# Two blocks of a weight matrix loaded by transfers over five and three DMA engines, in a decode step of attention and a gated MLP

## The chip, the cores and the metric

The kernel runs on one NeuronCore of a Trainium2 chip. Its engines are TensorE (PE in the profile, with its weight loads as PEld), VectorE (DVE), ScalarE (ACT), GpSimd (POOL) and SyncE (SP), which issues nearly all transfers. Sixteen DMA engines move the data. The metric is the device time of one execution in microseconds, and smaller is better.

## The reference

One decode step for eight sequences. All arrays are float32.

```python
xn = layernorm(x)                                  # x: [8, 1, 512]
q = (xn @ wq) -> 32 heads of 128                   # wq: [512, 4096]
scores = q . k_cache * 128 ** -0.5                 # k_cache: [8, 8, 4096, 128], 4 query heads share a k head
o = softmax(scores) @ v_cache                      # v_cache: as k_cache
s = o @ wo                                         # wo: [4096, 512]
z = gelu(xn @ w_in)                                # w_in: [512, 1792]
z1, z2 = z[..., :896], layernorm(z[..., 896:])
y = (z1 * (w_sp * z2 + b_sp)) @ w_out              # w_out: [896, 512]
out = x + s * silu(y)
```

The caches make up most of the bytes: 16 loads of 8.4 MB for each of k and v.

## The kernel before

**Loads.** Every load but x is one or more transfers from SP's queue, in the order of the program, and each fills all 128 partitions. A ring of three slots of 64 KB for each partition (pool `ring`, `slot()`) takes them: the first slot holds `w_mlp` (w_in, the seven blocks of w_out and small side values, line 59), the second wq (line 74), and then come the k and v loads of each head in two halves (`load_k`, line 288, `load_v`, line 295). At the end come wo in ten transfers (lines 322 and 325) and the last half of v in two. A load into a slot waits until all reads of the slot's last content are done. x is a transfer of eight rows from ACT's queue (line 71), into the columns of the MLP's slot that its load leaves free. `from_slot` gives out these columns, and the MLP's temporaries lie there too.

**Work.** First comes the layer norm of x and its transpose `xnT` (lines 122 to 130). Then `mlp()` runs: products with w_in into `pz` (line 145), gelu, layer norm and gate on DVE (lines 148 to 177), two transposes into `hT` (line 181), and seven products, one for each block of 128 rows of w_out (line 186). Each of the blocks goes to one of four groups of 32 rows in PSUM, which `pick` adds (line 193), and a silu leaves the result in `gate` (line 201). `project_q` makes the queries in two quads of heads (line 208) and spreads them into `qz` (line 220). For each head then `scores` (line 231), `softmax` (lines 236 to 259) and `values` (line 273) run, each half as it lands. After the last head the last pieces of wo are used as they land (line 307 and, straight into the result, line 354), and the result is stored from ACT's queue (line 368).

**What sets the order.** Instructions run on each engine in the order of the program text. Semaphores stand between engines. Nothing in the program says which DMA engine takes which row of a transfer.

Of the kernel before, what the change touches and what calls it, by code (L numbers as in the profile page):

```python
# [8 lines left out]
F32 = mybir.dt.float32  # L9
# [4 lines left out]
P = 128  # L14
B, D = 8, 512
HKV, REP, S, DH = 8, 4, 4096, 128
NK = D // P
G = 4
J = S // (G * P)
R = 32  # L20
FH = 896
FQ = 256
NB = FH // P
EPS = 1e-5
GELU_C = 0.7978845608028654
HALF = B // 2
# [2 lines left out]
W = 64  # L29
# [5 lines left out]


@with_exitstack
def tile_gqa_gmlp_decode(ctx: ExitStack, tc: tile.TileContext, x, kT, v, wq, wo, w_mlp, out, gate, stored):
    nc = tc.nc
    head = ctx.enter_context(tc.tile_pool(name="head", bufs=1))  # L40
    l = head.tile([P, HKV], F32, name="l")
# [5 lines left out]
    work = ctx.enter_context(tc.tile_pool(name="work", bufs=1))  # L47
# [4 lines left out]
    def slot():  # L52
        return ring.tile([P, SLOT], F32, name="slot")


    mlp_slot = slot()
    n_in, n_out = NK * 2 * FH, NB * D
    n_mlp = n_in + n_out + P
    nc.sync.dma_start(mlp_slot[:, :n_mlp], w_mlp)
    w_in_sb = mlp_slot[:, :n_in].rearrange("p (k n) -> p k n", k=NK)  # L60
    w_out_sb = mlp_slot[:, n_in:n_in + n_out].rearrange("p (j d) -> p j d", j=NB)
    side_sb = mlp_slot[:, n_in + n_out:n_mlp]
    spare = [n_mlp]

    def from_slot(rows, n):
        lo = spare[0]
        spare[0] = lo + n
        return mlp_slot[:rows, lo:lo + n]

    x_sb = from_slot(B, D)  # L70
    nc.scalar.dma_start(x_sb, x)

    wq_sb = slot()
    nc.sync.dma_start(wq_sb, wq)
    wq_sb = wq_sb.rearrange("p (k n) -> p k n", k=NK)


    ident = const.tile([P, P], F32, name="ident")
# [31 lines left out]
    def scratch(shape, name):  # L110
        t = ps.tile([P, 512], F32, name="scr")
        n = 1
        for s in shape[1:]:
            n *= s
        return t[:shape[0], :n]
# [16 lines left out]
    x_out = const.tile([P, W], F32, name="x_out")  # L132

    def mlp():
        z = from_slot(P, 2 * FQ).rearrange("p (a f) -> p a f", a=2)
        u = from_slot(P, 2 * FQ).rearrange("p (a f) -> p a f", a=2)
        pz = scratch([P, 2 * FQ], "pz")
        nc.vector.memset(pz, 0.0)
        pz_v = pz.rearrange("p (a f) -> p a f", a=2)
        w_in_v = w_in_sb.rearrange("p k (a f) -> p k a f", a=2)  # L140
        for k in range(NK):
            for g in range(G):
                lo = g * FQ
                n = min(FQ, FH - lo)
                nc.tensor.matmul(pz_v[R * g:R * (g + 1), :, :n], xnT[:, k, :],  # L145
                                 w_in_v[:, k, :, lo:lo + n], start=(k == 0), stop=(k == NK - 1))
        zf, uf = z.rearrange("p a f -> p (a f)"), u.rearrange("p a f -> p (a f)")
        nc.vector.tensor_copy(zf, pz)
        nc.vector.tensor_mul(uf, zf, zf)
        nc.vector.tensor_scalar(uf, uf, 0.044715, 1.0, op0=ALU.mult, op1=ALU.add)  # L150
        nc.vector.tensor_mul(uf, uf, zf)
        nc.scalar.activation(uf, uf, AF.Tanh, scale=GELU_C)
        nc.vector.tensor_scalar(uf, uf, 1.0, 0.5, op0=ALU.add, op1=ALU.mult)
        nc.vector.tensor_mul(zf, uf, zf)

        def mean(src, name):
            part_sum = small.tile([P, 1], F32, name="part_sum")
            nc.vector.tensor_reduce(part_sum, src, op=ALU.add, axis=AX.X)  # L158
            pm = scratch([P, 1], "pm")
            nc.tensor.matmul(pm, same_all, part_sum, start=True, stop=True)  # L160
            t = small.tile([P, 1], F32, name=name)
            nc.vector.tensor_scalar(t, pm, 1.0 / FH, None, op0=ALU.mult)
            return t

        z1, z2 = z[:, 0, :], z[:, 1, :]
        mu = mean(z2, "mu")
        nc.vector.tensor_scalar(z2, z2, mu, None, op0=ALU.subtract)
        nc.vector.tensor_mul(u[:, 0, :], z2, z2)
        nc.vector.memset(u[(G - 1) * R:, 0, FH - (G - 1) * FQ:], 0.0)
        var = mean(u[:, 0, :], "var")  # L170
        nc.vector.tensor_scalar(var, var, EPS, None, op0=ALU.add)
        rs = small.tile([P, 1], F32, name="rs")
        nc.gpsimd.tensor_tensor(rs, var, neg_half, op=ALU.pow)
        nc.vector.tensor_scalar(z2, z2, rs, None, op0=ALU.mult)
        nc.vector.tensor_scalar(z2, z2, side_sb[:, W:W + 1], side_sb[:, W + 1:W + 2],
                                op0=ALU.mult, op1=ALU.add)
        nc.vector.tensor_mul(u[:, 1, :], z2, z1)
        hT = from_slot(P, 2 * P).rearrange("p (a s) -> p a s", a=2)
        for a in range(2):
            th = scratch([P, P], "th")  # L180
            nc.tensor.transpose(th, u[:, 1, a * P:(a + 1) * P], ident)
            nc.vector.tensor_copy(hT[:, a, :], th)  # L182
        pw = scratch([P, D], "pw")
        for j in range(NB):
            g, a = divmod(j, 2)
            nc.tensor.matmul(pw[R * g:R * (g + 1), :], hT[:, a, R * g:R * (g + 1)], w_out_sb[:, j, :],  # L186
                             start=(a == 0), stop=(a == 1 or j == NB - 1))
        y_sb = from_slot(P, D)
        nc.vector.tensor_copy(y_sb, pw)  # L189
        py = scratch([P, W], "py")  # L190
        for g in range(G):
            for a in range(2):
                nc.tensor.matmul(py[R * g:R * (g + 1), :], pick[:, a, :],  # L193
                                 y_sb[:, (2 * g + a) * W:(2 * g + a + 1) * W], start=(a == 0), stop=(a == 1))
        nc.vector.tensor_copy(x_out, side_sb[:, :W])
        e = from_slot(P, W)
        nc.vector.tensor_scalar(e, py, -1.0, 87.0, op0=ALU.mult, op1=ALU.min)
        nc.scalar.activation(e, e, AF.Exp)
        nc.vector.tensor_scalar(e, e, 1.0, None, op0=ALU.add)
        nc.vector.reciprocal(e, e)  # L200
        nc.vector.tensor_mul(gate, py, e)

    def project_q(quad):
        pq = scratch([P, REP * DH], "pq")
        for k in range(NK):
            for g in range(G):
                lo = (quad * G + g) * REP * DH
                nc.tensor.matmul(pq[R * g:R * (g + 1), :], xnT[:, k, :], wq_sb[:, k, lo:lo + REP * DH],  # L208
                                 start=(k == 0), stop=(k == NK - 1))
        q_sb = work.tile([P, REP * DH], F32, name="q_sb", tag="p")  # L210
        nc.vector.tensor_scalar(q_sb, pq, float(DH) ** -0.5, None, op0=ALU.mult)  # L211
        tq = scratch([P, REP * P], "tq")
        for r in range(REP):
            nc.tensor.transpose(tq[:, r * P:(r + 1) * P], q_sb[:, r * DH:(r + 1) * DH], ident)  # L214
        tv = tq.rearrange("p (r g c) -> p r g c", r=REP, g=G)
        for g in range(G):
            h = quad * G + g
            for b in range(B):
                o = b * R + b * REP
                nc.vector.tensor_copy(qz[:, h, o:o + REP], tv[:, :, g, b])  # L220
# [86 lines left out]
                nc.tensor.matmul(part[R * q:R * q + B, i * n:(i + 1) * n], oT[:, h, r, :],  # L307
                                 wo_sb[:, m, i * n:(i + 1) * n], start=(m < REP), stop=(cuts == 2))

    mlp()  # L310
    project_q(0)
    project_q(1)
    for h in range(HKV):
        for half in range(2):
            scores(h, half, load_k(h, half))
        pT = softmax(h)
        po = po_ps[:, h % 2]
        for half in range(2):
            last = h == HKV - 1 and half == 1
            if last:  # L320
                wo_slot = slot()
                nc.sync.dma_start(wo_slot[:, :WO_EARLY * D], wo[:, :WO_EARLY * D])
                v_sb = load_v(h, half, 2)
                for lo, hi in WO_PIECES:
                    nc.sync.dma_start(wo_slot[:, lo * D:hi * D], wo[:, lo * D:hi * D])
                wo_sb = wo_slot.rearrange("p (m d) -> p m d", d=D)
                project_o(0, WO_EARLY)
            else:
                v_sb = load_v(h, half, 1)
            n = 2 if last else HALF  # L330
            for i in range(0, HALF, n):
                done = values(half * HALF + i, n, pT, v_sb[:, i:i + n])
                if half or i:
                    combine(*o_prev, po)
                o_prev = done
        combine(*o_prev, po)
        po_t = po.rearrange("p (b r) -> p r b", r=REP)
        if h < HKV - 1:
            nc.vector.tensor_copy(oT[:, h], po_t)
        else:  # L340
            for a in range(2):
                nc.vector.tensor_copy(oT_last[:, :, a, a * B:(a + 1) * B], po_t)
# [16 lines left out]
    for a in range(2):  # L359
        for g in range(G):  # L360
            c = (2 * g + a) * W
# [46 lines left out]
```

## Time and profile before

| | |
|---|---|
| three runs | 681.53, 681.62, 681.85 us (median 681.62) |
| the profiled execution's own time | 681.75 us |
| its span, first to last instruction | 680.3 us |
| granted TensorE clock, mean | 0.749 |
| PE, PEld, DVE, ACT, POOL busy | 50%, 13%, 13%, 2%, 1% of the span |
| read from HBM | 290.80 MB, 428 GB/s over the span |

The busy share of an engine is an average over the span. The chain of waits shows what ended last at each point, and windows of time show the transfers' share of the sixteen DMA engines in each stretch.

### The profile page before, as it was taken

How to read it: one execution, taken by the hardware profiler on the slowest of the kernel's cores; microseconds unless marked ns; L12 is line 12 of the kernel's file. 1: busy time of each engine (PE TensorE's matmuls, PEld its weight loads, DVE VectorE, ACT ScalarE, POOL GpSimd, SP SyncE). 2: the span in 40 equal slices, each digit the busy share in tenths (PEclk: the TensorE clock that was granted, in tenths of full speed). 3: DMA queues.
4: the chain of work that ended last, by engine and by line, in shares of the span. 5: the costliest groups of instructions: out<-in, count | busy, mean ns of one | idle time of the engine just before them, and what ended most of it. 6: DMA issues, size and time to landing. Idle time of an engine off the chain costs nothing.

```text
span 680.3 us, 5234 instructions
## 1 busy us (share of the span) xinstructions
PE 340.2 (50%) x2398; PEld 91.0 (13%) x2398; DVE 87.1 (13%) x228; ACT 13.4 (2%) x27; POOL 3.9 (1%) x12
## 2 busy tenths in 40 slices
PE   0484544336555444445554344455554444555557
PEld 0121111111111111111111011111111111111112
DVE  2431021102110021102101021101201021100121
ACT  0000000000000000000000000000000000000000
POOL 1000000000000000000000000000000000000000
PEclk9777666787876667788766677887766678787688
DMA  9999999999999999999999999999999999999996
GB/s 390 432 433 432 433 432 433 432 433 439 436 443 444 432 432 429 432 429 432 436 432 433 432 439 433 432 436 435 429 432 429 432 432 433 439 444 435 415 422 278
DMA packets 6662, 291.17 MB, mean 428 GB/s; under 512 B 872, under 2 KB 872, under 8 KB 1648
## 3 DMA queue, kind: packets, MB, share of 16 engines
q1 hardware_dynamic: 6480, 290.79, 98.9%
q8 instruction: 19, 0.31, 0.2%
q10 hardware_dynamic: 160, 0.05, 0.1%
q14 instruction: 3, 0.02, 0.0%
HBM read 290.80 MB, written 0.03 MB: 428 GB/s over the span
## 4 chain that ended last, share of the span: by engine, by line
DMA 79%; PE 15%; issue 4%; DVE 1%; another core or an unknown queue 1%; SPq 0%; POOL 0%; POOLq 0%
DMA slot<-in_kT 36%; DMA slot<-in_v 35%; DMA slot<-in_wo 7%; PE o_ps L273 7%; PE sc L231 7%; PE scr L208 1%; DMA slot<-in_x 0%; SPq L295 0%; DVE q_sb L211 0%; DVE slot L189 0%; DVE st L122 0%; PE scr L193 0%; PE scr L214 0%; POOLq L402 0%
## 5 line engine op out<-in xcount | busy, mean ns | idle before, releaser
L231 PE MATMUL sc<-slot,qz 128*32 128x512 f32 x1024 | 144.8, 729 | 143.3 <-DMA slot<-in_kT 143.3
L273 PE MATMUL o_ps<-slot,pT 128*16 128x512 f32 x1024 | 149.0, 746 | 114.6 <-DMA slot<-in_v 114.6
L231 PEld LDWEIGHTS sc<-slot,qz 128*32 128x32 f32 x1024 | 37.6, 131 | 244.2 <-issue 154.5
L273 PEld LDWEIGHTS o_ps<-slot,pT 128*16 128x16 f32 x1024 | 33.0, 114 | 216.5 <-issue 153.8
L236 DVE TENSOR_REDUCE nm<-sc 128x1 f32<-128x1024 f32 x8 | 9.8, 1224 | 284.8 <-PE sc L231 284.8
L276 DVE TENSOR_TENSOR o_all<-o_ps,diag 128x512 f32<-128x512 f32 x17 | 11.8, 691 | 249.1 <-PE o_ps L273 249.1
L238 ACT ACTIVATE p<-sc,nm 128x1024 f32<-128x1024 f32 x8 | 8.9, 1113 | 577.6 <-DVE nm L236 577.6
L283 PE MATMUL po_ps<-fold,o_sb 128*128 128x16 f32 x30 | 5.9, 273 | 26.8 <-DVE o_sb L278 26.8
L278 DVE TENSOR_REDUCE o_sb<-o_all 128x128 f32<-128x512 f32 x17 | 17.8, 1047 | 0.6
L145 PE MATMUL scr<-slot,xnT 128*32 128x512 f32 (+1 forms) x32 | 6.3, 876 | 9.9 <-DMA slot<-in_w_mlp 9.9
L259 DVE STREAM_TRANSPOSE pT<-p 128x1024 f32<-128x1024 f32 x8 | 10.0, 1246 | 0.3
L283 PEld LDWEIGHTS po_ps<-fold,o_sb 128*128 128x128 f32 x30 | 4.5, 188 | 40.6 <-DVE o_sb L278 40.6
L208 PE MATMUL scr<-slot,xnT 128*32 128x512 f32 x64 | 8.8, 698 | 0.0
L307 PE MATMUL sc<-slot,oT 128*8 128x512 f32 (+1 forms) x60 | 8.2, 565 | 0.8 <-DMA slot<-in_wo 0.8
L241 PE MATMUL scr<-ident,nm 128*1 128x128 f32 x8 | 2.2, 271 | 10.8 <-DVE nm L236 10.8
L254 PE MATMUL scr<-wl,same 128*128 128x1 f32 x16 | 3.2, 272 | 6.2 <-DVE wl L252 6.2
L257 DVE TENSOR_SCALAR p<-p,w 128x1024 f32<-128x1024 f32 x8 | 6.0, 753 | 0.3
L220 DVE COPY qz<-scr 128x4 f32<-128x4 f32 x64 | 4.6, 146 | 1.5 <-PE scr L214 1.5
L160 PE MATMUL scr<-part_sum,same 128*128 128x1 f32 x4 | 1.1, 348 | 7.0 <-DVE part_sum L158 7.0
L247 PE MATMUL scr<-ident,full 1*128 1x1 f32 x8 | 1.7, 214 | 5.1 <-DVE full L245 5.1
L186 PE MATMUL scr<-slot 128*32 128x512 f32 x14 | 3.9, 1060 | 0.2 <-DVE slot L182 0.2
L254 PEld LDWEIGHTS scr<-wl,same 128*128 128x128 f32 x16 | 2.8, 219 | 6.6 <-PE scr L247 6.6
(88 smaller groups left out, 57.0 us busy)
## 6 DMA issues: line engine op xcount, KB each, us to landing
slot<-in_v SPq DMA_DIRECT2D x2, 4096.0 KB, 30.6
slot<-in_w_mlp SPq DMA_DIRECT2D x1, 5440.0 KB, 15.4
slot<-in_wo SPq DMA_DIRECT2D x1, 2048.0 KB, 36.1
slot<-in_wo SPq DMA_DIRECT2D x1, 1536.0 KB, 38.4
slot<-in_wo SPq DMA_DIRECT2D x1, 1280.0 KB, 40.9
slot<-in_wo SPq DMA_DIRECT2D x1, 1024.0 KB, 42.9
slot<-in_wo SPq DMA_DIRECT2D x4, 256.0 KB, 18.6
slot<-in_wo SPq DMA_DIRECT2D x1, 768.0 KB
```

Of the source, the lines that this page charges most:

```text
L145: nc.tensor.matmul(pz_v[R * g:R * (g + 1), :, :n], xnT[:, k, :], w_in_v[:, k, :, lo:lo + n], start=(k == 0), stop=(k == NK - 1))
L208: nc.tensor.matmul(pq[R * g:R * (g + 1), :], xnT[:, k, :], wq_sb[:, k, lo:lo + REP * DH], start=(k == 0), stop=(k == NK - 1))
L231: nc.tensor.matmul(sc[R * g:R * (g + 1), c, :], qz[:, h, b * R:(b + 1) * R], k_sb[:, i, c, g, :], start=(b == 0), stop=(b == B - 1))
L236: nc.vector.tensor_reduce(m, sc, op=ALU.max, axis=AX.XY, negate=True)
L238: nc.scalar.activation(p, sc.rearrange("p c s -> p (c s)"), AF.Exp, bias=m, accum_out=l[:, h:h + 1])
L254: nc.tensor.matmul(tot, same_all, wl, start=True, stop=True)
L259: nc.vector.transpose(pT.rearrange("p j b g r -> p j g b r"), p.rearrange("p (j g b r) -> p j g b r", j=J, g=G, b=B))
L273: nc.tensor.matmul(of[R * c:R * c + G * REP, :], pT[:, j, b0 + i], v_sb[:, i, j], start=(j < rows), stop=(j >= J - rows))
L276: nc.vector.tensor_mul(o_all, o, diag[:, :, None].to_broadcast([P, G, DH]))
L278: nc.vector.tensor_reduce(o_sb, o_all.rearrange("p g d -> p d g"), op=ALU.add, axis=AX.X)
L283: nc.tensor.matmul(po[:, b0 * REP:(b0 + n) * REP], o_sb, f.rearrange("p i r -> p (i r)"), start=True, stop=True)
L307: nc.tensor.matmul(part[R * q:R * q + B, i * n:(i + 1) * n], oT[:, h, r, :], wo_sb[:, m, i * n:(i + 1) * n], start=(m < REP), stop=(cuts = ...
```

## The change

The blocks of w_out with numbers 1 and 3 (`moved`) leave `w_mlp`, whose rows become 4 KB shorter in each of 128 partitions. Their 256 rows of 2 KB go into two new arrays. The first, `w_ex0`, fills partitions 0 to 39: each partition gets two chunks of K for each of the two blocks, 8 KB in all. The second, `w_ex1`, fills partitions 0 to 23 in the same way, in columns of its own. In memory the first array is five groups of eight rows and the second three groups of eight, with an unused ninth row behind each group, so that a transfer can be split over five or three DMA engines and not over more. The bytes read stay the same.

The order on SP's queue becomes wq, x, `w_mlp`, the two new transfers, k. x moves from ACT's queue to SP's. `project_q` is called ahead of `mlp()`. In `mlp()` the transposed activations of the moved blocks are made by four more transposes, in pieces of 40 and 24 rows (`te`, `hE`), and the two products of the moved blocks become eight, of 40 or 24 rows, so that thirteen products stand where there were seven. Their order goes round the four groups. The temporaries of the MLP move from the slot into buffers that the softmax uses later.

```diff
+MOVED = 2
+CHUNKS = 2
+EXTRA = [5 * B, 3 * B]
...
+    wq_sb = slot()
+    nc.sync.dma_start(wq_sb, wq)
...
     mlp_slot = slot()
-    n_in, n_out = NK * 2 * FH, NB * D
+    n_in, n_out = NK * 2 * FH, (NB - MOVED) * D
...
-    nc.scalar.dma_start(x_sb, x)
...
+    nc.sync.dma_start(x_sb, x)
+    nc.sync.dma_start(mlp_slot[:, :n_mlp], w_mlp)
+    w_ex = []
+    for rows, src in zip(EXTRA, (w_ex0, w_ex1)):
+        t = from_slot(rows, MOVED * CHUNKS * D)
+        nc.sync.dma_start(t, src[:, :B])
+        w_ex.append(t.rearrange("p (g c d) -> p g c d", g=MOVED, c=CHUNKS))
...
+        te = scratch([EXTRA[0], 2 * P], "te")
+        moved = []
+        f, o, wide = P, 0, MOVED * R
+        for rows, t in zip(EXTRA, w_ex):
+            lo = o
+            for c in range(CHUNKS):
+                nc.tensor.transpose(te[:rows, o:o + wide], u[:wide, 1, f:f + rows], ident[:wide, :wide])
+                moved += [(hE[:rows, o + g * R:o + (g + 1) * R], t[:, g, c, :]) for g in range(MOVED)]
+                f += rows
+                o += wide
+            nc.vector.tensor_copy(hE[:rows, lo:o], te[:rows, lo:o])
         pw = scratch([P, D], "pw")
+        parts = [[] for _ in range(G)]
+        kept = 0
         for j in range(NB):
             g, a = divmod(j, 2)
-            nc.tensor.matmul(pw[R * g:R * (g + 1), :], hT[:, a, R * g:R * (g + 1)], w_out_sb[:, j, :],
-                             start=(a == 0), stop=(a == 1 or j == NB - 1))
+            if a == 0 or g >= MOVED:
+                parts[g].append((hT[:, a, R * g:R * (g + 1)], w_out_sb[:, kept, :]))
+                kept += 1
+        for m in moved:
+            min(parts, key=len).append(m)
+        for i in range(max(map(len, parts))):
+            for g in range(G):
+                if i < len(parts[g]):
+                    nc.tensor.matmul(pw[R * g:R * (g + 1), :], *parts[g][i],
+                                     start=(i == 0), stop=(i == len(parts[g]) - 1))
...
-    mlp()
     project_q(0)
     project_q(1)
+    mlp()
...
+    w_out = c(B_w_out).reshape(NB, P, D)
+    moved = list(range(1, 2 * MOVED, 2))
+    w_ex, f = [], 0
+    for n in EXTRA:
+        m = n // B
+        e = np.zeros((m, B + 1, MOVED, CHUNKS, D), np.float32)
+        e[:, :B] = w_out[moved, f:f + n * CHUNKS].reshape(MOVED, CHUNKS, m, B, D).transpose(2, 3, 0, 1, 4)
+        w_ex.append(e.reshape(m, B + 1, MOVED * CHUNKS * D))
+        f += n * CHUNKS
```

More of the change, by code (lines that the diff above doesn't have):

```diff
@@ L37, in tile_gqa_gmlp_decode @@
 @with_exitstack
-def tile_gqa_gmlp_decode(ctx: ExitStack, tc: tile.TileContext, x, kT, v, wq, wo, w_mlp, out, gate, stored):
+def tile_gqa_gmlp_decode(ctx: ExitStack, tc: tile.TileContext, x, kT, v, wq, wo, w_mlp, w_ex0, w_ex1, out, gate, stored):
     nc = tc.nc
@@ L53, in slot @@
         return ring.tile([P, SLOT], F32, name="slot")
+    wq_sb = slot()
+    nc.sync.dma_start(wq_sb, wq)
+    wq_sb = wq_sb.rearrange("p (k n) -> p k n", k=NK)
     mlp_slot = slot()
-    n_in, n_out = NK * 2 * FH, NB * D
+    n_in, n_out = NK * 2 * FH, (NB - MOVED) * D
     n_mlp = n_in + n_out + P
-    nc.sync.dma_start(mlp_slot[:, :n_mlp], w_mlp)
     w_in_sb = mlp_slot[:, :n_in].rearrange("p (k n) -> p k n", k=NK)
-    w_out_sb = mlp_slot[:, n_in:n_in + n_out].rearrange("p (j d) -> p j d", j=NB)
+    w_out_sb = mlp_slot[:, n_in:n_in + n_out].rearrange("p (j d) -> p j d", j=NB - MOVED)
     side_sb = mlp_slot[:, n_in + n_out:n_mlp]
@@ L70, in tile_gqa_gmlp_decode @@
     x_sb = from_slot(B, D)
[L71 to L75, printed above, removed]
+    nc.sync.dma_start(x_sb, x)
[5 more added lines that the diff above has]
+        w_ex.append(t.rearrange("p (g c d) -> p g c d", g=MOVED, c=CHUNKS))
     ident = const.tile([P, P], F32, name="ident")
@@ L134, in mlp @@
     def mlp():
-        z = from_slot(P, 2 * FQ).rearrange("p (a f) -> p a f", a=2)
-        u = from_slot(P, 2 * FQ).rearrange("p (a f) -> p a f", a=2)
+        zu = work.tile([P, 2, 2, FQ], F32, name="zu", tag="p")
+        z, u = zu[:, 0], zu[:, 1]
+        rest = work.tile([P, 2 * D], F32, name="rest", tag="pT")
+        hT, hE, y_sb = rest[:, :2 * P], rest[:, 2 * P:D], rest[:, D:]
+        hT = hT.rearrange("p (a s) -> p a s", a=2)
         pz = scratch([P, 2 * FQ], "pz")
@@ L177, in mlp @@
         nc.vector.tensor_mul(u[:, 1, :], z2, z1)
-        hT = from_slot(P, 2 * P).rearrange("p (a s) -> p a s", a=2)
         for a in range(2):
@@ L182, in mlp @@
             nc.vector.tensor_copy(hT[:, a, :], th)
+        te = scratch([EXTRA[0], 2 * P], "te")
[9 more added lines that the diff above has]
+            nc.vector.tensor_copy(hE[:rows, lo:o], te[:rows, lo:o])
         pw = scratch([P, D], "pw")
+        parts = [[] for _ in range(G)]
+        kept = 0
         for j in range(NB):
             g, a = divmod(j, 2)
-            nc.tensor.matmul(pw[R * g:R * (g + 1), :], hT[:, a, R * g:R * (g + 1)], w_out_sb[:, j, :],
-                             start=(a == 0), stop=(a == 1 or j == NB - 1))
-        y_sb = from_slot(P, D)
+            if a == 0 or g >= MOVED:
[8 more added lines that the diff above has]
+                                     start=(i == 0), stop=(i == len(parts[g]) - 1))
         nc.vector.tensor_copy(y_sb, pw)
@@ L195, in mlp @@
         nc.vector.tensor_copy(x_out, side_sb[:, :W])
-        e = from_slot(P, W)
+        e = work.tile([P, W], F32, name="e", tag="o_all")
         nc.vector.tensor_scalar(e, py, -1.0, 87.0, op0=ALU.mult, op1=ALU.min)
@@ L392 @@
             c(B_w_in).reshape(NK, P, 2 * FH).transpose(1, 0, 2).reshape(P, NK * 2 * FH),
-            c(B_w_out).reshape(NB, P, D).transpose(1, 0, 2).reshape(P, NB * D),
+            np.delete(w_out, moved, 0).transpose(1, 0, 2).reshape(P, (NB - MOVED) * D),
             side.reshape(P, P)], axis=1),
+        "w_ex0": w_ex[0],
+        "w_ex1": w_ex[1],
     }
```

## The prediction

> **What bounds the kernel now.** I read the page's DMA queues and chain first, then the windows of time, then the timeline at both ends, and last the packet records of the trace.
>
> ```profile
> span 680.3 us, 5234 instructions
> ...
> q1 hardware_dynamic: 6480, 290.79, 98.9%
> q8 instruction: 19, 0.31, 0.2%
> ...
> q14 instruction: 3, 0.02, 0.0%
> ...
> DMA 79%; PE 15%; issue 4%; DVE 1%; another core or an unknown queue 1%; SPq 0%; POOL 0%; POOLq 0%
> ```
>
> The loads (q1) keep the sixteen DMA engines 98.9% busy, and the chain that ended last is DMA for 79% of the span. So the time is what the slowest DMA engine needs for its rows, plus a short tail. The windows show the pace and, at the end, how unevenly the engines stop (columns: stretch and length, then the busy times of five engines, the clock, the DMA share and GB/s):
>
> ```profile
> core 0: us, PE busy (x) PEld busy (x) DVE busy (x) ACT busy (x) POOL busy (x), PEclk, DMA share, GB/s
> ...
> 93.00:640.00 547.00, 270.47 (x1864) 70.52 (x1868) 56.17 (x98) 9.85 (x21) 0.00 (x0) 0.73 1.00 433
> ...
> 672.00:673.00 1.00, 1.00 (x10) 0.17 (x8) 0.00 (x0) 0.00 (x0) 0.00 (x0) 1.00 1.00 397
> 673.00:674.00 1.00, 0.33 (x6) 0.11 (x6) 0.00 (x0) 0.00 (x0) 0.00 (x0) 1.00 0.63 244
> 674.00:675.00 1.00, 0.85 (x6) 0.00 (x0) 0.00 (x0) 0.00 (x0) 0.00 (x0) 1.00 0.54 209
> 675.00:676.00 1.00, 0.88 (x24) 0.39 (x24) 0.29 (x1) 0.00 (x0) 0.00 (x0) 1.00 0.43 166
> 676.00:677.00 1.00, 0.85 (x48) 0.52 (x40) 0.40 (x1) 0.00 (x0) 0.00 (x0) 1.00 0.13 49
> 677.00:678.00 1.00, 0.78 (x32) 0.43 (x32) 0.00 (x0) 0.00 (x0) 0.00 (x0) 1.00 0.02 6
> ```
>
> 433 GB/s over sixteen engines is 27.1 GB/s for one: 1.21 us for 32 KB, 0.302 us for an 8 KB row. Up to 673 us all sixteen work. Then the share is 0.54 (8.6 engines), 0.43 (6.9) and 0.13 (two). So about half of the engines stop at 673, six near 675.8 and two near 677.2. The shares from 673 on add up to 1.75 us of all sixteen: a perfect balance would end the loads at 674.75, 2.45 us earlier, which bounds any gain from moving bytes between engines.
>
> The packet records say why. Packets on one engine follow each other without a gap, so each engine's chain can be followed from its first packet to its last:
>
> ```
> instruction packets on the engine      engines   last packet ends, us
> none                                      6      672.8 to 673.1
> only 8 KB ones (q14)                      2      673.5, 674.6
> two of 16 KB (q8)                         6      675.6 to 675.9
> three of 16 KB (q8)                       2      677.1, 677.2
> ```
>
> The 19 packets of 16 KB on q8 (the last comes after the loads) go round eight engines in a fixed order, and each puts its engine back by about 1.4 us (0.6 us of its own bytes, the rest a gap and one slower packet). The other eight engines never carry one. Which physical engines they are the trace doesn't number. x's eight packets tell this much: of the eight engines that carry them (their first packet of `w_mlp` starts just behind x's) six carry no q8 packet, one carries two and one three.
>
> The tail behind the last landing:
>
> ```profile
> 677.58 0.42 PE L354 MATMUL acc<-slot,oT_last 128*16 128x64 f32 x16 [0.22 <-DMA slot<-in_wo]
> 678.07 0.23 DVE L366 TENSOR_TENSOR gate<-acc,gate 128x64 f32<-128x64 f32 x1 [1.67 <-PE acc L354]
> 678.33 0.23 DVE L367 TENSOR_TENSOR gate<-gate,x_out 128x64 f32<-128x64 f32 x1
> 678.58 0.38 ACTq L368 DMA_DIRECT2D out<-gate  x1
> ```
>
> It doesn't change, so a shift of the last landing (677.2) is a shift of the time. The profiled execution took 681.75 us, 0.13 above the median of 681.62.
>
> **Bytes of each engine.** A full load gives each engine eight rows. Every engine loses 8 x 4 KB of `w_mlp`: -1.21 us. The first new transfer gives five engines 8 rows of 8 KB each, +2.42 us; the second gives three engines the same. I take both to begin at the first engine, so the first three carry both: -1.21 + 4.84 = +3.63 us. The fourth and fifth: +1.21. The other eleven: -1.21. x now stands in the queue of eight engines (2 KB, +0.08). [...]
>
> At full pace, and if the first three are among those that stopped at 673.0, they end at 673.0 + 3.71 = 676.7, the worst q8 engines at 677.2 - 1.2 = 676.0, and the time falls by 0.5 us to 681.1.
>
> **The unknown price: many engines writing few partitions.** In the kernel before every big load lets each engine write eight partitions of its own, 27.1 GB/s each. The new transfers go to partitions 0 to 39 while the engines that are done with `w_mlp`, or carry no part of these transfers, already write k into all 128. Whether a partition takes bytes from two engines at full pace the long loads can't show. The one transfer to few partitions is x, sixteen KB over eight engines into eight partitions:
>
> ```profile
> 0.74 2.44 DMA slot<-in_x
> ...
> slot<-in_x ACTq DMA_DIRECT2D x1, 16.0 KB
> ```
>
> Landing took 2.44 us. Of its 2 KB packets two took 0.08 us, the full pace, and six 0.45 to 1.11 us. The engines were then also at their first packets of `w_mlp`, which were slow everywhere, so this isn't proof. Bounds for the first three engines: 0, if nothing is shared, and 4.84 us more, if every moved byte goes at half pace beside another writer. A gain is excluded, since no packet in the trace went faster than 27.1 GB/s. I take three quarters, 3.63 us, because x, the nearest row, lies at the slow end and because the last of three engines decides, not their mean. Then the first engine ends at 676.7 + 3.6 = 680.3, which is 3.1 us behind 677.2: 681.62 + 3.1 = 684.7 us by the median, 684.85 for an execution like the profiled one.
>
> [...]
>
> **What is hidden: the start.** Does the new order starve the queue? The rows:
>
> ```profile
> 0.74 0.37 SPq L59 DMA_DIRECT2D slot<-in_w_mlp  x1
> 0.74 0.57 ACTq L71 DMA_DIRECT2D slot<-in_x  x1
> 1.16 0.42 SPq L74 DMA_DIRECT2D slot<-in_wq  x1
> 1.63 39.69 SPq L288 DMA_DIRECT2D slot<-in_kT  x2
> 3.20 0.68 DVE L122 BATCH_NORM_STATS2 st<-slot 8x6 f32<-8x512 f32 x1 [1.07 <-DMA slot<-in_x]
> 6.42 0.19 DVE L130 COPY xnT<-scr 128x32 f32<-128x32 f32 x1
> 16.15 0.20 DVE L195 COPY x_out<-slot 128x64 f32<-128x64 f32 x1 [9.54 <-DMA slot<-in_w_mlp]
> 16.26 6.26 PE L145 MATMUL scr<-slot,xnT 128*32 128x512 f32 x32 [9.88 <-DMA slot<-in_w_mlp]
> 33.03 0.69 PE L181 MATMUL scr<-ident,slot 128*128 128x128 f32 x2 [2.38 <-DVE slot L177]
> 33.89 3.85 PE L186 MATMUL scr<-slot 128*32 128x512 f32 x14 [0.17 <-DVE slot L182]
> 38.99 5.16 PE L208 MATMUL scr<-slot,xnT 128*32 128x512 f32 x32
> 45.55 3.64 PE L208 MATMUL scr<-slot,xnT 128*32 128x512 f32 x32
> ```
>
> SP's issues cost 0.4 us each and all of the first six wait for nothing, so k's first half is queued by about 4 us. `w_mlp`'s 5.57 MB need 12.9 us at 433 GB/s and landed at 16.15, so loads count from 3.3 us. After: wq (8.39 MB, 19.4 us) lands at 22.7, x at 22.8, `w_mlp` (5.05 MB, 11.7 us) at 34.4; an engine without new rows is done with the first half of k at 53.8.
>
> The second half of k needs wq's slot. x to `xnT` takes 3.4 us (3.18 to 6.61), both quads 10.2 us (38.99 to 49.19): issued at 36.4, 17 us before it is needed. The layer norm, once hidden under `w_mlp`'s load, is now hidden under the queued one. On DVE the MLP now stands behind the queries' copies, on PE behind their transposes: it begins at 38.
>
> The first half of v needs the MLP's slot, and SP's queue stands still behind that wait. From line 145's start to line 186's end it was 21.5 us (16.26 to 37.74). Six more products go through line 186's work: 12 of its 14 matmuls again, 3.3 us, and four transposes and two copies some 1.9 us. So the slot is free at 38 + 21.5 + 5.2 = 64.7; the fastest engines need the load at 53.8 + 19.4 = 73.2. 8.5 us of cover; the load's issue to first byte (0.74 to about 1.8) takes one. The new rows land at 34.4 + 8.5 at the latest, before they are used. Were the cover gone, each us late would cost the fast engines one us, of which the slow ones hide the first four. I cost the whole start at nothing.
>
> Later, a slot is free some 10 us after a load lands and two loads of 19.4 us stand queued, so engines may lie over 25 us apart; 10 is the most expected. The last piece of wo is issued when the first of the nine has landed (line 325's issues end at 666.8, for a use at 677); a slow engine delays it by up to 3 us, and only engines that end early anyway notice.
>
> ```profile
> 637.18 29.61 SPq L325 DMA_DIRECT2D slot<-in_wo  x5
> ```
>
> **Rivals.**
> 1. *Nothing is shared, the balance works* (not slower). Then the end is 676.7, 681.1 us; between 680.9 and 682.7 if the 674.6 engine is among the first three or a q8 engine is the fourth or fifth (677.2 + 1.3 = 678.5). It decides if writers don't meet. For it: both ends of the sum lie at full pace. Against: x. Chance 0.27.
> 2. *A q8 engine among the first three, nothing shared.* 675.9 + 3.7 or 677.2 + 3.7: 684.0 to 685.3. For it: x shows two q8 engines among eight. Chance 0.08. With sharing besides, 687 to 689, which is inside the forecast's chance but above the range (0.1).
> 3. *The change doesn't do what it says*: the second transfer uses other engines than the first. Eight engines get 1.2 us more. If none of them is a q8 engine the end is 676.0, 680.4 us; if one is, 678.5. Chance 0.06.
> 4. *v's first half is late.* The MLP takes over 8 us longer than worked out; up to 4 us is hidden. Chance 0.04, half of it slower.
>
> **How the numbers follow.** Sharing has 0.55, all of it slower; its own range is 683.5 (half of the bytes slow: 679.1) to 686.0 (all: 681.5). About 0.2% (1.36 us) is what a measurement of this kernel can tell from no change. Slower: 0.55 + 0.08 + 0.02 = 0.65. Same: most of rival 1 and parts of 3 and 4, 0.28. Faster: what is left of 1 and 3, 0.07. The range reaches from rival 1 (681.0) to the upper end of sharing on the engine that stopped at 673.5 (686.5); out are rival 3's best case and sharing on a q8 engine, together under 0.2.
>
> **What would show it.** Right: the new transfers land over 5 us behind `w_mlp`; packets of k on the engines next to them take over 2.42 us around 35 to 45 us; at the end a few engines stop near 680 and the others at 672 to 676, so the DMA share falls to 0.2 or less for some 4 us. Wrong: the new 8 KB packets take 0.30 us each, and the share stays high until 676. The start is right if v's first load is issued near 65 us and the share is 1.0 from 16 to 640 us.

## The result and the profile after

The changed kernel took 685.14 us (median of four runs, 684.95 to 685.34), beside 681.74 us for the kernel before (four runs, 681.53 to 681.96): a ratio of 1.0050, 95% interval 1.0038 to 1.0063. It is slower by 3.4 us. The profiled execution took 685.34 us with a span of 683.8 us.

The page of the changed kernel, in the lines that answer to those of before:

```profile
span 683.8 us, 5273 instructions
...
q1 hardware_dynamic: 6568, 290.80, 98.9%
q8 instruction: 19, 0.31, 0.2%
...
DMA 79%; PE 16%; issue 4%; DVE 0%; SPq 0%; POOLq 0%; POOL 0%
```

Nothing here looks wrong: the same bytes, the queue as busy as before (98.9%), the chain as much DMA. A DMA engine counts as busy while its packet is slow (a share of 1.08 at 315 GB/s below). What these lines cannot show, GB/s by stretch shows (windows of time; the columns are stretch and length, five engines' busy times, the clock, the DMA share, GB/s). First the changed kernel, then two stretches of the kernel before:

```profile
core 0: us, PE busy (x) PEld busy (x) DVE busy (x) ACT busy (x) POOL busy (x), PEclk, DMA share, GB/s
28.00:33.00 5.00, 4.17 (x26) 0.97 (x19) 0.69 (x1) 0.00 (x0) 0.00 (x0) 1.00 0.95 410
33.00:43.00 10.00, 8.25 (x72) 2.77 (x70) 6.63 (x69) 0.00 (x0) 0.00 (x0) 1.00 1.08 315
43.00:48.00 5.00, 0.00 (x0) 0.00 (x0) 2.85 (x5) 1.91 (x2) 0.00 (x0) 0.62 0.97 419
93.00:640.00 547.00, 272.68 (x1851) 71.56 (x1851) 58.80 (x104) 10.29 (x24) 0.00 (x0) 0.72 1.00 433
...
675.00:676.00 1.00, 1.00 (x10) 0.40 (x14) 0.29 (x2) 0.00 (x0) 0.00 (x0) 1.00 0.84 336
676.00:677.00 1.00, 1.00 (x14) 0.29 (x8) 0.00 (x0) 0.00 (x0) 0.00 (x0) 1.00 0.84 332
677.00:678.00 1.00, 1.00 (x13) 0.21 (x8) 0.00 (x0) 0.00 (x0) 0.00 (x0) 1.00 0.73 285
678.00:679.00 1.00, 1.00 (x13) 0.12 (x8) 0.00 (x0) 0.00 (x0) 0.00 (x0) 1.00 0.40 156
679.00:680.00 1.00, 0.80 (x24) 0.27 (x16) 0.55 (x1) 0.00 (x0) 0.00 (x0) 1.00 0.25 96
680.00:681.00 1.00, 0.97 (x48) 0.71 (x48) 0.14 (x1) 0.00 (x0) 0.00 (x0) 1.00 0.06 25
```
```profile
33.00:38.00 5.00, 4.54 (x16) 1.41 (x16) 0.69 (x3) 0.00 (x0) 0.00 (x0) 0.50 0.97 419
38.00:43.00 5.00, 4.43 (x40) 1.59 (x44) 1.70 (x5) 0.26 (x1) 0.00 (x0) 0.59 0.95 410
```

From 33 to 43 us, while the two new transfers run, the engines are all busy and move 315 GB/s, where the kernel before has 410 to 419. From 93 to 640 us the pace is the 433 of before. (A packet is counted where it starts, so single shares can pass 1.) At the end the engines stop between 675 and 681 us.

The timeline of the start and the tail:

```profile
3.69 33.66 SPq L317 DMA_DIRECT2D slot<-in_kT  x2
...
22.78 0.68 DVE L129 BATCH_NORM_STATS2 st<-slot 8x6 f32<-8x512 f32 x1 [19.35 <-DMA slot<-in_x]
...
38.49 3.63 PE L155 MATMUL scr<-slot,xnT 128*32 128x512 f32 x32
...
681.30 0.42 PE L383 MATMUL acc<-slot,oT_last 128*16 128x64 f32 x16 [0.22 <-DMA slot<-in_wo]
...
682.05 0.23 DVE L396 TENSOR_TENSOR gate<-gate,x_out 128x64 f32<-128x64 f32 x1
682.31 0.37 ACTq L397 DMA_DIRECT2D out<-gate  x1
```

x lands at 22.78 us, the MLP begins at 38.49, and the second half of k is issued at 37.35 (3.69 + 33.66). The tail is the one of before, moved from 677.2 to 680.97 us (the last landing in the packet records).

The packet records of both kernels, on the sixteen engines (us from the span's start; a 64 KB packet of k is one partition's row, 2.42 us at full pace):

```
                              first two k packets   first half of k done     last packet done
before, engines without q8    2.42  2.42            54.0 to 54.4 (one 55.1)  672.8 to 673.1 (q14: 673.5, 674.6)
after, eleven engines         3.9-4.4  3.6-3.8      56.0 to 56.9 (one 58.6)  674.7 to 675.5, with q8 677.6 to 680.1
after, fourth and fifth       4.0-4.4 (after 8 KB)  58.9, 59.5 (q14)         679.0 (q14) and below
after, first three            (behind 16 rows)      61.1, 61.2, 62.3         679.7, 679.8, 680.97
new 8 KB packets              from 0.31 (full pace) to 0.69 us, over half of them 0.55 or more
```

The two odd ones (55.1 and 58.6) had just carried an instruction packet. The engines that are only loading k, which have nothing to do with the new transfers, run at 0.55 to 0.67 of full pace (2.42 us against 3.6 to 4.4) until these end at 42.7 us. What an engine has lost by 43 us is what it is late by at the end: nothing is made up in between.

### The profile page after: what moved, and what is told of

Its sections match the earlier page's. It is cut to its first block, busy times and chain, and to the rows that moved or that the text cites. A ratio compares the mean times of both kernels' runs of the same rounds, so it can differ in the third digit from the quotient of the medians.

```text
span 683.8 us, 5273 instructions
## 1 busy us (share of the span) xinstructions
PE 351.1 (51%) x2414; PEld 92.3 (14%) x2414; DVE 88.0 (13%) x230; ACT 13.4 (2%) x27; POOL 3.9 (1%) x12
## 3 DMA queue, kind: packets, MB, share of 16 engines
q1 hardware_dynamic: 6568, 290.80, 98.9%
## 4 chain that ended last, share of the span: by engine, by line
DMA 79%; PE 16%; issue 4%; DVE 0%; SPq 0%; POOLq 0%; POOL 0%
DMA slot<-in_kT 35%; DMA slot<-in_v 33%; DMA slot<-in_wo 7%; PE sc L260 7%; PE o_ps L302 7%; DMA slot<-in_x 3%; PE scr L216 2%; SPq L324 0%; PE scr L198 0%; DVE st L129 0%; POOLq L442 0%; POOL rstd L132 0%; PE scr L190 0%; PE acc L383 0%; DVE zu L187 0%
## 5 line engine op out<-in xcount | busy, mean ns | idle before, releaser
L260 PE MATMUL sc<-slot,qz 128*32 128x512 f32 x1024 | 147.9, 742 | 130.5 <-DMA slot<-in_kT 130.5
L216 PE MATMUL scr<-slot,rest 128*32 128x512 f32 (+2 forms) x26 | 11.2, 1058 | 0.0
```

Of the source, the lines that this page charges most:

```text
L216: nc.tensor.matmul(pw[R * g:R * (g + 1), :], *parts[g][i], start=(i == 0), stop=(i == len(parts[g]) - 1))
L260: nc.tensor.matmul(sc[R * g:R * (g + 1), c, :], qz[:, h, b * R:(b + 1) * R], k_sb[:, i, c, g, :], start=(b == 0), stop=(b == B - 1))
```

## The experiments

The first question was which part costs: the order, or the new transfers; the second, whether the transfers cost by where they write. The letters e1 to e13 name the runs (there is no e6); in each diff `EXTRA` gives, for each transfer, the engines, the rows of an engine and the chunks of K, and `BASES` the first partition.

**e1, the order alone.** w_out stays whole in `w_mlp`; wq, x, `w_mlp`, k and the queries ahead of the MLP are as in the changed kernel.

```diff
-MOVED = 2
-CHUNKS = 2
-EXTRA = [5 * B, 3 * B]
+MOVED = 0
+EXTRA = []
+BASES = []
...
```

> All blocks of w_out stay in the MLP's load; only the order of the loads (wq, x, MLP, k) and of the work (queries ahead of the MLP) is that of the change. Both theories price the order at nothing: 681.4 to 682.2 us, and no packet of k over 2.45 us around 35 to 45 us. A time above 683 would put part of the loss on the order.

Measured: 681.72 us (ten runs, 681.52 to 682.18), beside 681.75 for the kernel before, ratio 1.0000 (0.9991 to 1.0009). k's packets stayed at 2.42 us, but for one of 2.95 that begins where an instruction packet of q14 ended. The order costs nothing that can be measured, and the loss belongs to the two transfers and what uses them.

**e2, each engine's rows in its own partitions.** The edit takes it, as an assumption of mine, that in the long loads one engine writes four neighbouring partitions and the four that lie 32 higher. For the places used here the runs bear this out: rows so placed took 0.611 us for 16 KB (e8), four rows in 96 to 99 slowed one other engine (4.28 us for a packet of k in e10), and four in 20 to 23 with four in 52 to 55 also one (6.48 us in e13). So in e2 each of five engines gets four rows of 16 KB in partitions 0 to 19 and each of three the same in 32 to 43: the bytes on each engine stay, and the places change.

```diff
-CHUNKS = 2
-EXTRA = [5 * B, 3 * B]
+EXTRA = [(5, 4, 4), (3, 4, 4)]
+BASES = [0, 32]
...
+        t = here[b0:b0 + m * per, :MOVED * chunks * D]
...
+        pw2 = scratch([R, D], "pw2")
+        for i, m in enumerate(other):
+            nc.tensor.matmul(pw2, *m, start=(i == 0), stop=(i == len(other) - 1))
...
```

> [...] Theory W (two engines writing the same partitions hinder each other, and the stall spreads): no packet slows, the last engine ends near 676.7, 681.0 to 681.7 us. Theory R (the slowing comes from the few engines or from reading the small arrays, wherever the rows land): 684.5 to 685.5 us as the change.

Measured: 687.28 us (687.08 to 687.41), ratio 1.0080 (1.0063 to 1.0096). That is above both expected ranges, and the time alone would have killed the theory of the places, but the trace shows two things at once. Every new packet took 0.611 us, full pace for 16 KB, no packet of k was slowed but the two behind instruction packets, and the eleven other engines had the first half of k at 52.8 to 53.4 us (one, behind an instruction packet, at 54.5). The loss came later. First the timeline, then a window:

```profile
66.12 11.30 PE L226 MATMUL scr<-slot,zu 12*32 12x512 f32 x13
...
77.45 10.45 SPq L334 DMA_DIRECT2D slot<-in_v  x2
```
```profile
70.00:76.00 6.00, 6.00 (x8) 1.20 (x7) 0.00 (x0) 0.00 (x0) 0.00 (x0) 0.50 0.35 153
```

My split needed 21 products, eight of them into one PSUM group; a product is two matmuls, and the last thirteen of the sixteen stand one behind the other, 0.87 us each. The MLP's slot came free at 77.45 us, when the engines had needed v's first load from about 72.5 on (53.1 + 19.4), and from 70 to 76 us the DMA share was 0.35. That is the prediction's fourth rival, met in my own experiment; e5 and e8 therefore have a shorter MLP.

**e3, one transfer over all sixteen engines.** The same rows, spread over every engine, into partitions 0 to 63.

```diff
-CHUNKS = 2
-EXTRA = [5 * B, 3 * B]
+EXTRA = [(64, 1, 2)]
+BASES = [0]
...
```

> The same 512 KB as one transfer of 64 rows over all sixteen engines into partitions 0 to 63, so each engine has as many bytes as before the change. Theory W: sixteen engines write into the partitions of eight, so the stretch takes about twice its 1.2 us and k's first packets are slowed too: 682.7 to 684 us. Theory R (few engines): full pace, 681.4 to 682.2 us.

Measured: 683.26 us (ten runs, 682.92 to 683.60), ratio 1.0022 (1.0012 to 1.0031). Here every engine has the bytes of before, so the balance can't explain the 1.5 us beside e1. The first thirteen of the 8 KB packets took 0.31 us and most others 0.5 to 0.65, the first packets of k 2.7 to 3.4, and the first half of k came 1.5 us later than in e1. That is the whole loss, and it is what the theory of the places expects.

**e4, e2 with the rows 64 partitions higher.** By the same assumption partitions 64 to 83 and 96 to 107 belong to other engines in the long loads.

```diff
-BASES = [0, 32]
+BASES = [64, 96]
```

> As the run with own partitions, but the rows land 64 partitions higher (64 to 83 and 96 to 107), so that each of the five engines writes where another one of the sixteen is just writing k. Theory W: packets of k slow as in the change for as long as the rows last, 683 to 686 us. Theory R: as the change too, 684.5 to 685.5 us; only the pair with the run on own partitions tells them apart.

Measured: 686.32 us (685.82 to 688.34), just above both ranges, ratio 1.0072 (1.0056 to 1.0088). Most of the new packets took 1.2 to 1.3 us, twice those of e2, and the first two k packets on all eleven other engines 4.2 to 5.0 us. From 70 to 76 us the share is 1.06: everybody was so late that the slow MLP hardly starved them. e2 and e4 so lose about the same time by two different ways, and only their packets tell them apart.

**e5, e2 with a shorter MLP.** Chunks of both transfers share a product (64 partitions, the gaps filled with zeros), so that thirteen products stand as in the changed kernel, and x and its normed copy leave the slot. In this run the columns of the moved weights were taken in another order, so the moved part of y is another sum of the same size.

```diff
-    x_sb = from_slot(B, D)
+    x_sb = work.tile([P, D], F32, name="x_sb", tag="o_all")[:B]
...
+        nc.vector.memset(hE[:2 * R], 0.0)
...
+            rows = 2 * R if c < EXTRA[1][2] else EXTRA[0][0] * EXTRA[0][1]
...
+                moved.append((hE[:rows, c * wide + g * R:c * wide + (g + 1) * R], here[:rows, o:o + D]))
...
```

> Rows and engines as in the run with own partitions, but each product takes the rows of both transfers together (thirteen products as in the change, not twenty-one), so that the MLP's slot is free near 67 us, before the fast engines need it at 72. x and its layer norm lie outside the slot to make room. Theory W (rows that an engine writes where no other writes run at full pace): no packet slows, the first three engines end at 676.7, the engines with three instruction packets at 676.0, 681.0 to 681.5 us, a little faster than before. If the loss came from few engines or small arrays after all (R): 684.5 or more. If the run with own partitions was slow for another reason than its late slot: 686 to 687.

Measured: 680.99 us (eleven runs, 680.82 to 681.12) beside 681.89, ratio 0.9986 (0.9977 to 0.9995). With the places put right, the change that was slower by 3.4 us is faster by 0.9.

**e7, two engines at foreign places.** e5 (its order of columns too) and one more transfer, whose data nothing uses: the first two engines write 64 KB more each, into partitions 96 to 103, where by the same assumption two other engines write k.

```diff
+        if b0 != BASES[0]:
+            nc.sync.dma_start(here[96:104], w_cross[:, :4])
...
```

> As the run before it, plus one unused transfer: the first two engines each write 64 KB more, into partitions 96 to 103, where two other engines write k. [...] If a conflict anywhere slows all sixteen, as the run with rows 64 partitions higher looked: k's packets take 3.5 us or more on all fourteen other engines, 683.5 to 685.5 us.

Measured: 685.66 us (one run), a little above the expected range. The extra packets took 1.23 to 1.25 us from the second on. I had thought that two pairs of engines would pay. But all fourteen other engines had one k packet of 3.9 to 4.3 us and one of 2.8 to 3.3; the extra packets ran from 38.6 to 43.0 us.

**e8 and e9, the pair that differs in the place alone.** e8 is e5 with the columns in the reference's order; e9 is e8 with rows and activations 64 partitions higher, with the same products and the same bytes on each engine.

```diff
-                o = (c * MOVED + g) * D
+                o = (g * EXTRA[0][2] + c) * D
```
```diff
-BASES = [0, 32]
+BASES = [64, 96]
...
```

> The run on own partitions with thirteen products once more, with the columns of the moved weights taken in the order in which they lie. The transfers are the same: 680.8 to 681.3 us, 0.1% below before.

> [...] If a conflict at any partition slows all sixteen engines to half while it lasts: the 4.84 us of new rows take 9.7, every engine loses up to 4.8 us, the first three end at 681.5 and the time is 685.5 to 686.5. [...] If nothing is shared: 681.

Measured: e8 680.93 us (eleven runs, 680.87 to 681.13) beside 681.65, ratio 0.9989 (0.9981 to 0.9998); e9 686.09 us (four runs, 685.85 to 686.16), ratio 1.0062 (1.0047 to 1.0078). The place alone is worth 5.2 us. The windows, first of e8, then of e9:

```profile
33.00:43.00 10.00, 8.19 (x72) 2.71 (x69) 6.69 (x69) 0.00 (x0) 0.00 (x0) 1.00 0.98 420
...
674.00:675.00 1.00, 0.77 (x11) 0.12 (x8) 0.00 (x0) 0.00 (x0) 0.00 (x0) 1.00 0.64 248
675.00:676.00 1.00, 0.77 (x39) 0.52 (x39) 0.69 (x1) 0.00 (x0) 0.00 (x0) 1.00 0.37 141
676.00:677.00 1.00, 0.81 (x44) 0.46 (x32) 0.00 (x0) 0.00 (x0) 0.00 (x0) 1.00 0.11 41
```
```profile
33.00:43.00 10.00, 8.52 (x72) 3.04 (x72) 6.33 (x69) 0.00 (x0) 0.00 (x0) 1.00 1.08 256
...
676.00:677.00 1.00, 1.00 (x10) 0.12 (x8) 0.00 (x0) 0.00 (x0) 0.00 (x0) 1.00 0.92 375
...
681.00:682.00 1.00, 0.78 (x43) 0.43 (x32) 0.00 (x0) 0.00 (x0) 0.00 (x0) 1.00 0.14 43
```

The engines and the bytes are the same, the DMA share near 1 in both: 420 GB/s against 256. In e9 every engine's first k packets took 4.2 to 5.0 us. The first three carry eight packets of 16 KB each; at 1.25 us for all of them these would lose 8 x (1.25 - 0.61) = 5.1 us, and the first ones were faster. The last packet ended at 676.70 us in e8 and at 681.48 in e9, 4.8 us later; the two profiled executions (681.06 and 685.85 us) lie as far apart.

**e10, one engine at one foreign place.** e8 and four unused transfers of one row, into partitions 96 to 99.

```diff
+        if b0 != BASES[0]:
+            for i in range(4):
+                nc.sync.dma_start(here[96 + i:97 + i, :MOVED * EXTRA[0][2] * D], w_cross[i:i + 1])
...
```

> The previous version with each engine's rows in its own partitions (680.93 us), plus four unused transfers of one row of 16 KB each into partitions 96 to 99, issued between the two new ones. I expect all four on the first engine, whose own partitions those are not: 64 KB more there, 2.4 us at full pace. Theory 'any conflict halves all engines': the four packets take about 1.23 us each, and the k packets of all fifteen other engines that fall in that stretch (some 5 us) take 3.8 us or more in place of 2.42, so that k's first half lands 2 to 2.5 us later on every engine. Theory 'only the two that meet pay': the four packets take 1.23 us, one other engine has k packets over 3 us, and fourteen stay at 2.42. Theory 'it takes two conflicts at once, or more': nothing slows, 0.61 us for each of the four. The first engine ends at 676.7 + 2.4 + 2.4 in the first two theories, 681.5, so 685.7 us, and at 679.1 in the third, 683.3 us; if the four rows go to four engines, each pays 0.6 to 1.2 us and the time is 681.5 to 682.5 us.

**e12 and e13, two engines, at two places or at one.** As e10, with two rows in each transfer, one from each of the first two engines: into 96 + i and 100 + i in e12 (e7's places in e10's form), into 20 + i and 52 + i in e13.

```diff
-                nc.sync.dma_start(here[96 + i:97 + i, :MOVED * EXTRA[0][2] * D], w_cross[i:i + 1])
+                nc.sync.dma_start(here[96 + i:101 + i:4], w_cross[:, i])
...
```
```diff
-                nc.sync.dma_start(here[96 + i:101 + i:4], w_cross[:, i])
+                nc.sync.dma_start(here[20 + i:53 + i:32], w_cross[:, i])
```

> [...] The form is that of the run with one engine (several small transfers), the places are those of the run with one transfer of eight rows. Theory 'two places at once slow all, one place only its pair': the packets take about 1.23 us and the k packets of all fourteen others 3.8 us or more for some 4 us. Theory 'the form of the transfer decided': the packets take 1.23 us, two other engines have k packets near 4.3, and twelve stay at 2.42 to 2.5. The first two engines end at 676.7 + 2.4 + 2 to 2.4 = 681.1 to 681.5, so 685.3 to 685.8 us by both; the packets decide.

> As the run before, but the two rows of each transfer go to partitions 20 + i and 52 + i, which in the long loads one engine writes, so that three engines meet at one place. Theory 'each place that is met costs only those who meet there, until two places are met': the new packets take 1.83 us each (a third of the pace) while all three write, one other engine has a k packet over 6 us, thirteen stay at 2.42 to 2.5; the first two end at 676.7 + 7.3 = 684, so 688 us. Theory 'two engines that write elsewhere slow all': all fourteen others go to 3.8 us or more. Theory 'these two partitions are not at one place': 0.61 us or 1.23 us each.

Measured, one run each: 685.60, 685.90 and 688.22 us (685.7, 685.3 to 685.8 and 688 were expected by the theories with a meeting; the kernel before beside them: 681.78 for e10, 681.41 for the other two). In each, the engines that carry the extra bytes end last (one in e10, two in the others). The packets tell the theories apart (us; the k packets are those that fall into the conflict):

```
       new packets, 16 KB       the engine whose place it is   the other engines' k packets
e10    0.61 1.25 1.24 1.25      4.28, 2.93                     2.42 to 2.50 (one 3.14)
e12    0.61 1.30 1.30 1.30      4.0 to 4.6, 2.6 to 3.3         4.0 to 4.6, 2.6 to 3.3
e13    0.80 2.00 1.98 1.97      6.48, 3.59                     2.6 to 2.7, 2.9, 2.8 to 2.9 (two 3.4)
```

The packet of 3.14 us in e10 begins at 41.05 us, where an instruction packet of q14 ended; behind such a packet e1 and e8 have one of 2.95 us. The two of 3.4 us in e13 also stand behind instruction packets (q14 and q8).

The last column of windows says the same, from 38 to 48 us, for e10, e12 and e13 in this order:

```profile
38.00:48.00 10.00, 4.29 (x36) 1.68 (x36) 6.24 (x41) 1.91 (x2) 0.00 (x0) 0.87 0.99 409
```
```profile
38.00:48.00 10.00, 3.75 (x34) 1.26 (x32) 6.38 (x41) 1.91 (x2) 0.00 (x0) 0.95 0.99 325
```
```profile
38.00:48.00 10.00, 3.54 (x33) 1.34 (x24) 5.85 (x33) 1.91 (x2) 0.00 (x0) 0.88 1.07 376
```

One engine at one foreign place: the two that meet there share its pace (1.25 us for 16 KB in place of 0.61), and the rest pay up to 3% (at most 2.50 us in place of 2.42, but for the packet of 3.14). Two at one place: three share it (1.98 us is nearly a third of the pace), and the rest pay 7 to 20% (2.6 to 2.9 us), where k packets of 2.42 to 2.5 us were expected. Two at two places: every engine falls to 0.52 to 0.61 of its pace (4.0 to 4.6 us). The form of the transfers, one of eight rows in e7 (685.66 us) or four of two rows in e12 (685.90), made hardly a difference: one packet of k on each of the fourteen others took 3.9 to 4.3 us in e7 and 4.0 to 4.6 in e12.

**e11, another split.** e8 with 96 KB on each of five engines and 16 KB more on the first two, so that no engine has more than 112 KB; seventeen products.

```diff
-EXTRA = [(5, 4, 4), (3, 4, 4)]
+EXTRA = [(5, 4, 6), (2, 4, 1)]
...
```

> The version with each engine's rows in its own partitions, but split so that five engines get 96 KB each (partitions 0 to 19, six chunks of K of 20 rows) and the first two 16 KB more (partitions 32 to 39, one chunk of 8 rows); seventeen products in place of thirteen. If engines pay for bytes alone, the first two end at 673.0 + 3.6 + 0.6 - 1.2 = 676.0, the third to fifth at 675.4 (the one with the instruction packets of q14 at up to 677.0), the engines with three instruction packets at 676.0: 680.2 to 681.3 us, beside 680.93 for the split 128/64 KB and 681.7 before. The load of v's first half is issued up to 4 x 0.85 us later than at 66.9, before 70.5, still ahead of the 72.2 at which the first engine needs it. If instead the wait for the MLP is what these versions pay for, the time is 1 to 3 us above 680.93.

Measured: 681.38 us (eleven runs, 681.28 to 681.75) beside 681.78, ratio 0.9994 (0.9985 to 1.0003), just above the expected range. v's first half was issued at 68.0 us, in time. One engine ended at 677.04 us, the next at 676.2. By the sum, which the trace can't confirm since it doesn't number the engines, the late one is the engine of the five that also has the packets of q14; it ate what the smaller share of the first three gained. e8 is the best version found.

## Why the prediction was right, and where it was not

**The time and the last engine: right.** 684.7 was forecast and 685.14 measured; the profiled execution took 685.34 against 684.85. The last landing moved from 677.2 to 680.97 us, worked out as 680.3, and it is on one of the first three engines. None of the first three carries a packet of q8: from the first half of k to the end they took 618.6 us each, as the engines without such a packet did. The second rival stood on one that does.

**The bytes and the balance: right, borne out by e8.** That the two transfers use five and three engines, the three being among the five, was taken for granted in the sum; the packet records of the changed kernel show it, with sixteen 8 KB packets on three engines, eight on two more and none on the other eleven. At full pace the sum gave 676.7 us for the first three and 681.1 for the time. With the slowing taken away and the bytes left, the last packet ended at 676.70 and the time was 680.93. So the first rival was the true account of the bytes, and its condition, that writers don't meet, is the one thing that the change breaks.

**The price of the meeting: the size right on the engines that count.** The three engines had the first half of k at 61.1 to 62.3 us. Before it was 54.0 to 54.4; with 3.71 of bytes that is 57.9 (the last three engines of e8 have 57.6 to 57.9), so the meeting cost 3.2 to 4.4 us, and 3.63 was taken. It rested on three quarters of the way between two bounds, for which x's packets were the only row, so the size was a fair guess and not a measurement.

**The step that failed: who pays.** I had the cost on the engines that carry the new rows and on "the engines next to them", and the other eleven at 672 to 676 us, 1.2 earlier than before. In fact none of the sixteen was spared for 9 us: the eleven, at 0.55 to 0.67 of their pace, had the first half of k at 56.0 to 56.9 us (one at 58.6), where e8 has 52.7 to 53.3, and they ended at 674.7 to 675.5 without q8 packets and at up to 680.1 with them. The engine with three of those ended only 0.9 us ahead of the last, so with a little less on the first three it would have set the time. It was luck that this error did not reach the time: the first three were still later. In the same way "the DMA share falls to 0.2 or less for some 4 us" did not come: it was still 0.40 at 678, 0.25 at 679 and 0.06 at 680 us. A smaller misreading had no weight: there is no gap at an instruction packet. In both kernels the packet itself takes 0.88 to 1.01 us and the long one behind it 2.89 to 2.97, which is the 1.4 us of the prediction.

**The places.** Rows in the places that an engine also writes in the long loads go at full pace (e8, 0.611 us for 16 KB), rows 64 higher do not (e9, about 1.25), and 20 + i and 52 + i meet (e13, 1.98 us with three writers). If each place were shared by itself, engines at other places would keep their pace. e10 nearly bears that out (2.42 to 2.50 us) and e12 contradicts it (4.0 to 4.6 us on all fourteen). That 96 to 99 and 100 to 103 are two places is my assumption, after the groups of four rows in e8; no run shows it by itself.

**The start: right.** The MLP began at 38.49 us (38 forecast), the second half of k was issued at 37.35 (36.4), v's first half at 66.72 (64.7), and no engine ran dry (DMA share 0.99 from 48 to 90 us and 1.00 from 93 to 640). e1 shows the order's price on its own as nothing. The cover was real but not wide: e2's MLP freed the slot at 77.45 us, 5 us after the engines needed it, and its last packet ended 6.2 us behind that of e8.

**What stays open.** Why two foreign places slow all engines and one does not, is not settled. The runs show that the number of places counts more than the number of writers (e12 against e13, one run each) and that the form of the transfer does not. The source alone can't do it, since e8 reads the same arrays as e9 at full pace (0.611 us for 16 KB); whether it takes part, the records don't tell.

## What to carry to other kernels

When a kernel runs at the pace of its DMA engines, let a small transfer over few engines give every engine the partitions that it also writes in the long loads running beside it: here the change with such places gained 0.7 us, and the same rows 64 partitions higher cost 5.2 us more. Look for such a slowing in GB/s and in the time of one packet, since a slow packet counts as a busy engine and the DMA share stays near 1 (0.98 at 420 GB/s in e8, 1.08 at 256 in e9). And when an experiment moves bytes to other places, keep the consumers' instruction count, or the buffer that they free late will lose as much by another way (e2 687.28 us, e8 680.93).

## What the hardware showed that I had not expected

Two engines that each write at one place of another's slow all sixteen to little more than half their pace for as long as it lasts (k's packets take 4.0 to 4.6 us in e12 in place of 2.42), while one engine alone slows hardly more than the one that it meets (4.28 us there, at most 2.50 on the others in e10, but for the packet behind an instruction packet). The 16 KB instruction packets of q8 go to eight of the sixteen engines in turn, and in the changed kernel none of the first three is among them (engines without such packets end at 672.8 to 674.6 us in the kernel before, those with them at 675.6 to 677.2); this is why moving bytes to the first engines could gain anything, 0.7 us in e8.
